# Forty-four tiny loads added to a decode kernel that streams its KV cache

## The chip, the cores and the metric

The kernel runs on one core of a Trainium2 chip. The metric is device time in microseconds (us); lower is better. The kernel before takes 1275.87 us (median of three runs, 1275.85 to 1275.99). Five engines run their own instruction streams: TensorE (PE in the profile, with PEld for its weight loads), VectorE (DVE), ScalarE (ACT), GpSimd (POOL) and SyncE (SP). Data moves between main memory and the on-chip SBUF through 16 DMA engines; a load is issued by an instruction on one of the five engines and announces its landing by raising a semaphore by 16.

## The reference, cut to what matters

One token of an attention block with a long cache and one token of a gated feed-forward block are computed from the same input and mixed by a gate:

```python
x = A_x                                                   # 1 x 1 x 448
g = sigmoid((x * gate_w).sum(-1, keepdims=True))
q = (x @ wq)                                              # 16 heads of 256
scores = einsum("bhqd,bhkd->bhqk", q, k) * 256 ** -0.5    # 65536 cached keys, 8 KV heads
a = (softmax(scores) @ v) @ wo                            # 16*256 -> 448
b = ((relu(x @ W_gate)) * (x @ W_up)) @ W_down
return g * a + (1 - g) * b
```

The K cache and the V cache are 8 heads x 65536 x 256 values in bfloat16 each, 268 MB each. Everything else together is some 12 MB. So nearly all that the kernel does is to read 537 MB once.

## The kernel before, in words

K and V are read in tiles of 128 partitions x 32768 values (64 KB in a partition, 8.4 MB in all). There are 32 K tiles and 32 V tiles, four of each for a KV head; K tile `n` belongs to head `n // 4`. Three SBUF buffers, `ring0` to `ring2`, hold them. K tiles go alternately to `ring1` and `ring2`, V tiles to `ring0`; the last V tiles also use `ring1` and `ring2`, and the very last one comes in three pieces (`vp`, line 776).

All of these loads, and those of the weights, are issued by SyncE, in one fixed order (the list `order`): K0, `wq`, K1, `W_down`, K2, the gate and up weights, K3, and then K4, V0, K5, V1 and so on in pairs. The V tile `n - 4` stands right behind the K tile `n`. At the end stand the last V tiles, the three pieces of V31, six loads of `wo` in falling size (line 785), and the store of the output (line 798).

What a tile goes through:

- A K tile lands; VectorE transposes it in place in four pieces (line 529); TensorE multiplies it with the query into a PSUM bank `ST` (line 540, in two halves, `qk[n, 0]` and `qk[n, 1]`); VectorE takes the maximum (line 703), ScalarE the exponential (line 705). When `qk[n, 1]` is done, the buffer is free, and SyncE may issue K tile `n + 2` into it (line 680).
- A V tile lands; ScalarE copies the probabilities that belong to it (`pcur`, line 591); TensorE multiplies (line 584, `pv[n]`) into the PSUM bank `O`. When `pv[n]` is done, SyncE may issue the next V tile into `ring0` (line 772).

The order of the work is written by hand. Each operation has an engine, a key (a planned time) and the operations on which it depends; each engine's program is its operations sorted by key (`_Plan.finish`), and a dependency becomes a wait on a semaphore in front of the instruction (`_Plan.emit`). An instruction that waits holds all that stand behind it on its engine. `l_["xm"]` is the spread-out query, an early operation on VectorE. `scr` is a scratch tile of 128 x 1024 values that is used in the first 50 us only. GpSimd builds constants in the first 7 us and then has nothing left to do.

Of the kernel before, what the change touches and what calls it, by code (L numbers as in the profile page):

```python
# [27 lines left out]
class _Plan:  # L28
# [8 lines left out]
    def op(self, eng, key, fn, deps=(), tag=None):  # L37
        eng, cls = {"pv": ("pe", "pv"), "dx": ("dv", "dx"), "ap": ("ac", "ap")}.get(eng, (eng, eng))
        o = _Op(eng, key, fn, deps, tag=tag, cls=cls)
        self.ops.append(o)  # L40
        return o

    def dma(self, eng, key, sem, fn, deps=()):
        if sem not in self.dsem:
            self.dsem[sem] = self.es.enter_context(self.nc.semaphore("d_" + sem))
        o = _Op(eng, key, fn, deps, dma=sem)
        self.ops.append(o)
        return o
# [212 lines left out]
def bass_gated_mix__gqa_block_cached__glu_gated_reglu__decode_kernel(  # L261
# [35 lines left out]
    with es:  # L297
# [7 lines left out]
        scr = sb("scr", [128, 1024], BF)  # L305
        xcur = sb("xcur", [128, 136], BF)
        xm = sb("xm", [128, H * 128 + 8], BF)
# [32 lines left out]
        fin_o = P_sb[0:1, 0:D]  # L340
# [30 lines left out]
        op, dma = pl.op, pl.dma  # L371
# [23 lines left out]
        t = 3.0  # L395
# [5 lines left out]
        T_END = t + 20.0  # L401
# [115 lines left out]
        def k_src(n):  # L517
            h, t_ = divmod(n, NTH)
            return A_k_cache[0, h, t_ * TK:(t_ + 1) * TK, :].rearrange("(p u) d -> p (u d)", u=U)

        def v_src(i):
            h, a = divmod(i, NTH)
            return A_v_cache[0, h, :, :].rearrange("(t g p u) d -> g p t (u d)", t=NTH, g=NTH, u=U)[a]
# [37 lines left out]
        l_, qk, smax, aexp, pv, pc, last, first = {}, {}, {}, {}, {}, {}, {}, {}  # L561
        pending = []

        def free(key):
            out_ = []
            for f in freed[key]:
                out_.append(l_[f] if isinstance(f, str) else qk[f[1], 1] if f[0] == "k" else pv[f[1]])
            return out_
# [55 lines left out]
        for kind, i, t in sorted(issue, key=lambda q: q[0] != "wq"):  # L624
# [51 lines left out]
            elif kind == "k":  # L676
                n = i
                h, t_ = divmod(n, NTH)
                sl = slot["k", n]
                kd = dma("sp", t, "r%d" % sl, lambda e, n=n, sl=sl: e.dma_start(ring[sl][:], k_src(n)), free(("k", n)))  # L680
                tk = max(tL["k", n], last.get("free", 0))
                tr = [op("dv", tk + 4.5 * w, f_trans(sl, w), [kd]) for w in range(4)]
# [25 lines left out]
                if t_ == NTH - 1:  # L708
# [18 lines left out]
                    for rd in range(2):  # L727
# [10 lines left out]
                        p = op("pe", tt + 0.5, f_ptr, [rsc, g_idb], tag=("ptr", rd))  # L738
# [29 lines left out]
            elif kind in ("v", "vp"):  # L768
                if kind == "v":
                    n, lo, hi = i, 0, U  # L770
                    sl = slot["v", n]
                    dep = dma("sp", t, "r%d" % sl, lambda e, sl=sl, n=n: e.dma_start(ring[sl][:], v_src(n)), free(("v", n)))
                else:
                    n, (lo, hi) = NT - 1, PIECES[i]
                    sl = slot["vp", 0]
                    dep = dma("sp", t, ("wq", "wqh", "wd")[i], lambda e, sl=sl, n=n, lo=lo, hi=hi: e.dma_start(  # L776
                        ring[sl][:, lo * 256:hi * 256], v_src(n)[:, :, lo * 256:hi * 256]), free(("vp", 0)))
                args = (n, lo, hi, sl, tL[kind, i], dep)
                if ("tev", n // NTH) in last:
                    make_pv(*args)  # L780
                else:
                    pending.append(args)
            elif kind == "wo":
                lo, hi = WO[i]
                l_["wo", i] = dma("sp", t, "wo%d" % i, lambda e, lo=lo, hi=hi: e.dma_start(  # L785
                    wo_sb[:, lo:hi, :], A_wo.rearrange("(p s) n -> p s n", s=32)[:, lo:hi, :]), free(("wo", 0)))

# [7 lines left out]
            fin = op("pv", max(LAST + 0.5 + i, tL["wo", i]), f_wo, [l_["wo", i], aA, l_["dn"]])  # L795
        f0 = op("dx", T_END, lambda e: e.tensor_copy(fin_o[:, 0:D2], A_ps[0:1, 0:D2]), [fin])
        f1 = op("ap", T_END, lambda e: e.copy(fin_o[:, D2:D], A_ps[32:33, 0:D2]), [fin])
        f2 = dma("sp", T_END + 1, "out", lambda e: e.dma_start(out[0, :, :], fin_o), [f0, f1])

        pl.serialize(touch_m)  # L800
        for o in touch_m:
# [74 lines left out]
```

## Time and profile before

| what | value |
|---|---|
| median of three runs | 1275.87 us (1275.85 to 1275.99) |
| span of the profiled execution, first to last instruction | 1274.3 us |
| what the device time has around that span | some 1.6 us |
| TensorE busy | 365.9 us (29%) |
| VectorE busy | 630.1 us (49%) |
| ScalarE busy | 78.0 us (6%) |
| GpSimd busy | 4.6 us |
| bytes read | 549.03 MB, 431 GB/s over the span |
| mean granted TensorE clock | 0.634 |

The profile's page gives busy times, a strip of the span in 40 slices, the DMA queues, the chain of work that ended last, and the costliest groups of instructions. `SPq` is the time in which SyncE issues a load: a row `SPq L772` tells of the instruction that starts a transfer, not of the transfer. `q1` is the queue of the loads that SyncE issues; its packets are single runs of data and the small writes that raise a semaphore. `DMA ring<-in_A_v_cache_dram` in the chain is time in which the next step waited for a V tile to land.

### The profile page before, as it was taken

The page shows a single profiled execution, that of the slowest core. Times are in us where ns is not written, and L with a number is a line of the kernel's source. Part 1 is how long each engine was busy: PE and PEld are TensorE (multiplying, and loading weights), DVE is VectorE, ACT ScalarE, POOL GpSimd, SP SyncE. Part 2 cuts the span into 40 slices and gives each one's busy share as a digit, 9 for nine tenths or more (in the row PEclk, how much of TensorE's full clock was granted, in tenths as well). Part 3 has the DMA queues.
Part 4 walks back from the last instruction along what each step waited for, and adds up shares of the span by engine and source line. Part 5 has one row for each costly group of instructions (what it writes and reads, how often), then busy time and mean ns, then how long its engine had stood idle before and what let it go on. Part 6 is the DMA issues. An engine that isn't in the chain of part 4 may idle for free.

```text
span 1274.3 us, 10240 instructions
## 1 busy us (share of the span) xinstructions
PE 365.9 (29%) x4497; PEld 151.4 (12%) x4505; DVE 630.1 (49%) x309; ACT 78.0 (6%) x163; POOL 4.6 (0%) x23
## 2 busy tenths in 40 slices
PE   0534321133320332312233222323302332112525
PEld 0101110011110111101111110111100111001201
DVE  4777655553455633557433565335654355553300
ACT  0001100010000100001000010000000010000100
POOL 1000000000000000000000000000000000000000
PEclk9766665666655666656666656666566666566667
DMA  9999999999999999999999999999999999999998
GB/s 411 430 436 432 426 430 434 432 443 432 430 432 432 434 442 430 430 434 430 438 438 430 430 434 430 440 438 428 430 434 430 444 434 428 430 436 430 442 421 369
DMA packets 11389, 549.13 MB, mean 431 GB/s; under 512 B 1267, under 2 KB 1654, under 8 KB 2294
## 3 DMA queue, kind: packets, MB, share of 16 engines
q1 hardware_dynamic: 11378, 549.03, 99.7%
q8 instruction: 4, 0.07, 0.0%
q14 instruction: 3, 0.02, 0.0%
q10 hardware_dynamic: 4, 0.00, 0.0%
HBM read 549.03 MB, written 0.00 MB: 431 GB/s over the span
## 4 chain that ended last, share of the span: by engine, by line
DMA 81%; PE 16%; DVE 2%; ACT 1%; issue 1%; SPq 0%; ACTq 0%
DMA ring<-in_A_v_cache_dram 74%; PE O L584 13%; DMA ring<-in_A_wo_dram 3%; DMA ring<-in_A_wq_dram 2%; DMA ring<-in_A_k_cache_dram 2%; DVE ring L529 1%; PE ST L540 1%; ACT pcur L591 1%; PE O L501 1%; PE A_ps L551 0%; SPq L785 0%; SPq L776 0%; PE O L653 0%; DVE ring L660 0%; PE A_ps L653 0%
## 5 line engine op out<-in xcount | busy, mean ns | idle before, releaser
L529 DVE STREAM_TRANSPOSE ring<-ring 128x4096 uint32<-128x4096 uint32 x128 | 557.6, 4413 | 196.9 <-DMA ring<-in_A_k_cache_dram 196.9
L584 PE MATMUL O<-ring,pcur 128*4 128x512 bf16 x2048 | 187.3, 545 | 790.4 <-ACT pcur L591 781.9
L703 DVE TENSOR_REDUCE nmb<-ST 128x1 f32<-128x512 f32 x32 | 22.1, 692 | 345.9 <-PE ST L540 345.9
L584 PEld LDWEIGHTS O<-ring,pcur 128*4 128x4 bf16 x2048 | 59.3, 111 | 914.8 <-ACT pcur L591 794.6
L540 PE MATMUL ST<-ring,xcur 128*16 128x512 bf16 x2048 | 136.7, 420 | 44.3 <-DVE ring L529 43.7
L540 PEld LDWEIGHTS ST<-ring,xcur 128*16 128x16 bf16 x2048 | 62.4, 92 | 112.1 <-DVE ring L529 48.6
L705 ACT ACTIVATE P_sb<-ST,nmb 128x512 bf16<-128x512 f32 x32 | 44.6, 1392 | 368.3 <-DVE nmb L703 368.3
L591 ACT COPY pcur<-ptp 128x256 bf16<-128x256 bf16 x32 | 13.2, 415 | 732.6 <-DMA ring<-in_A_v_cache_dram 732.6
L607 DVE TENSOR_SCALAR o_sb<-O,rcm 128x256 bf16<-128x256 f32 x8 | 3.8, 479 | 61.1 <-PE O L584 61.1
L730 DVE TENSOR_TENSOR P_sb<-P_sb,hs 128x1024 bf16<-128x1024 bf16 x16 | 18.9, 1222 | 8.1 <-ACT hs L724 8.1
L735 PE MATMUL PT<-identb,P_sb 128*128 128x128 bf16 x128 | 14.5, 282 | 17.6 <-DVE P_sb L730 17.3
L501 PE MATMUL O<-ring,P_sb 128*128 128x512 bf16 x28 | 8.5, 477 | 17.3 <-DMA ring<-in_A_wq_dram 17.3
L735 PEld LDWEIGHTS PT<-identb,P_sb 128*128 128x128 bf16 x128 | 10.7, 127 | 19.9 <-DVE P_sb L730 19.9
L744 ACT COPY ptp<-PT 128x256 bf16<-128x256 bf16 x32 | 10.3, 375 | 23.0 <-PE PT L735 23.0
L705 ACT ACTIVATION_READ_ACCUMULATOR P_sb<-ST,nmb 128x1 f32 x32 | 8.3, 258 | 0.0
L501 PEld LDWEIGHTS O<-ring,P_sb 128*128 128x128 bf16 x28 | 3.2, 117 | 22.2 <-issue 20.5
L551 PE MATMUL A_ps<-ring,attnA 128*1 128x224 bf16 x64 | 5.3, 322 | 1.1 <-DMA ring<-in_A_wo_dram 1.0
L719 PE MATMUL M_ps<-identf,hs 128*2 128x128 f32 x8 | 2.3, 283 | 10.0 <-DVE hs L717 10.0
L756 DVE RECIPROCAL rc<-M_ps 128x2 f32<-128x2 f32 x8 | 1.4, 171 | 7.5 <-PE M_ps L755 7.5
L755 PE MATMUL M_ps<-hs,ones_f 128*128 128x2 f32 x16 | 4.5, 352 | 0.0
L722 PE MATMUL M_ps<-mx,nselT 2*128 2x1 f32 x16 | 3.2, 268 | 3.0 <-DVE mx L721 3.0
L755 PEld LDWEIGHTS M_ps<-hs,ones_f 128*128 128x128 f32 x16 | 4.0, 311 | 0.0
(93 smaller groups left out, 68.6 us busy)
## 6 DMA issues: line engine op xcount, KB each, us to landing
ring<-in_A_v_cache_dram SPq DMA_DIRECT2D x1, 4096.0 KB, 22.1
ring<-in_A_wq_dram SPq DMA_DIRECT2D x1, 3072.0 KB, 28.9
ring<-in_A_v_cache_dram SPq DMA_DIRECT2D x1, 3072.0 KB, 28.8
ring<-in_B_W_down_dram SPq DMA_DIRECT2D x1, 1568.0 KB, 53.0
ring<-in_B_W_gate_dram SPq DMA_DIRECT2D x1, 1344.0 KB, 26.3
ring<-in_B_W_up_dram SPq DMA_DIRECT2D x1, 1344.0 KB, 29.2
ring<-in_A_wo_dram SPq DMA_DIRECT2D x1, 1232.0 KB, 33.0
ring<-in_A_v_cache_dram SPq DMA_DIRECT2D x1, 1024.0 KB, 30.7
```

The lines of the kernel that those rows point to most:

```text
L501: ins = e.matmul(QN_ps, xw3[:, kt, 31 - m:159 - m], rhs, start=(kt == 0 and m == 0), stop=(kt == R3 and m == J // 4 - 1))
L529: return lambda e: e.transpose(v, v)
L540: ins = e.matmul(bank[32 * w:32 * w + 16, :], xcur[:, x0:x0 + 16], ktv[sl][:, u0:u0 + 16, c, :, r_], start=(b == 0 and c == 0 and r_ == 0) ...
L551: ins = e.matmul(A_ps[32 * g:32 * g + 1, 0:D2], lhsT, rhs[:, g * D2:(g + 1) * D2], start=start, stop=stop, skip_group_check=True, tile_pos ...
L584: ins = e.matmul(OP[32 * g:32 * g + 4, :], pcur[a % 2][:, 4 * k:4 * k + 4], ring[sl][:, k * 512:(k + 1) * 512], start=False, stop=False, s ...
L591: pc[n] = op("ap", max(tp - 5, last["tev", h] - 0.5), lambda e: e.copy(pcur[a % 2][:].rearrange("p (k i) -> p k i", i=4), ptp[:].rearrange ...
L703: smax[n] = op("dv", sx, lambda e, n=n, t_=t_: e.tensor_reduce(NM[:, t_:t_ + 1], ST[n % 2][:], AX.X, ALU.max, negate=True), [qk[n, 1], las ...
L705: aexp[n] = op("ac", sx + 1, lambda e, n=n, t_=t_: e.activation(P_sb[:, t_:2048:4], ST[n % 2][:], ACTF.Exp, bias=NM[:, t_:t_ + 1], scale=1 ...
L730: rsc = op("dv", tt, lambda e, pb=pb: e.tensor_tensor(pb, pb, X[:, 12:16].unsqueeze(1).to_broadcast([128, 256, 4]), ALU.mult), [h7, aexp[n]])
L735: ins = e.transpose(PT[rd][:, s * 128:(s + 1) * 128], P_sb[:, (rd * 8 + s) * 128:(rd * 8 + s + 1) * 128], identb[:, :])
L744: ins = e.copy(dst, src)
L755: l3 = mop("pe", T + 19, lambda e: e.matmul(LS_ps, ones_f[:, :], X[:, 6:8], start=True, stop=True), [l2, c_one], tag="l3")
```

## The change

Forty-four small loads are added, all from `B_W_gate` into `scr`, which nothing reads any more by then.

- Fifteen by SyncE just ahead of K8, the ninth K tile. Load `j` (1 to 15) takes `j` partitions of `32 + 2j` values: 68 to 124 bytes in a partition. They wait for `xm`.
- Fourteen by GpSimd, behind its last constant. They wait for `qk[9, 1]` and `xm`. Each takes 2 partitions (three of them 3, 5 and 8), two separate runs of 200 to 252 bytes in each.
- Fifteen more by SyncE, like the first, between the last piece of V31 and the first load of `wo`. The first of them waits until the earlier fifteen have landed.
- The store of the output gets two more waits, for the second fifteen and for GpSimd's fourteen.

SyncE's program around K8, before (the names are buffers and inputs; `[waits ...]` names the semaphores waited for, `s_pe` and `s_pv` those of TensorE):

```order
L680 DMA ring2<-in_A_k_cache_dram 128x32768 [waits s_pe]
L772 DMA ring0<-in_A_v_cache_dram 128x1x32768 [waits s_pv]
L680 DMA ring1<-in_A_k_cache_dram 128x32768 [waits s_pe]
L772 DMA ring0<-in_A_v_cache_dram 128x1x32768 [waits s_pv]
L680 DMA ring2<-in_A_k_cache_dram 128x32768 [waits s_pe]
```

The first two rows are K7 and V3, the third is K8. The same place now, where line 689 is the new one, 691 the K loads and 783 the V loads:

```order
L691 DMA ring2<-in_A_k_cache_dram 128x32768 [waits s_pe]
L783 DMA ring0<-in_A_v_cache_dram 128x1x32768 [waits s_pv]
L689 DMA scr<-in_B_W_gate_dram 1x34 [waits s_dx]
L689 DMA scr<-in_B_W_gate_dram 2x36
L689 DMA scr<-in_B_W_gate_dram 3x38
...
L689 DMA scr<-in_B_W_gate_dram 14x60
L689 DMA scr<-in_B_W_gate_dram 15x62
L691 DMA ring1<-in_A_k_cache_dram 128x32768 [waits s_pe]
L783 DMA ring0<-in_A_v_cache_dram 128x1x32768 [waits s_pv]
```

So K8 is issued behind fifteen more instructions, and the small loads stand in SyncE's queue between the data of V3 and that of K8.

The end of SyncE's program before, from the last piece of V31 on:

```order
L776 DMA ring2<-in_A_v_cache_dram 128x1x4096
L785 DMA ring0<-in_A_wo_dram 128x4928
L785 DMA ring0<-in_A_wo_dram 128x3136
L785 DMA ring0<-in_A_wo_dram 128x2240
L785 DMA ring0<-in_A_wo_dram 128x1792
L785 DMA ring0<-in_A_wo_dram 128x1344
L785 DMA ring0<-in_A_wo_dram 128x896
L798 DMA out_0_dram<-P_sb 1x448 [waits s_ap,s_dx]
```

The same place now:

```order
L787 DMA ring2<-in_A_v_cache_dram 128x1x4096
L799 DMA scr<-in_B_W_gate_dram 1x34 [waits d_probe]
L799 DMA scr<-in_B_W_gate_dram 2x36
...
L799 DMA scr<-in_B_W_gate_dram 15x62
L801 DMA ring0<-in_A_wo_dram 128x4928
L801 DMA ring0<-in_A_wo_dram 128x3136
L801 DMA ring0<-in_A_wo_dram 128x2240
L801 DMA ring0<-in_A_wo_dram 128x1792
L801 DMA ring0<-in_A_wo_dram 128x1344
L801 DMA ring0<-in_A_wo_dram 128x896
L814 DMA out_0_dram<-P_sb 1x448 [waits d_probe,d_probe1,s_ap,s_dx]
```

All six `wo` loads stand behind fifteen more instructions, and the store has two more waits. On TensorE, VectorE and ScalarE no instruction moves; on GpSimd the fourteen loads stand behind all that it had.

```diff
                 sl = slot["k", n]
+                if n == 11:
+                    for j, k_ in enumerate((2, 2, 2, 2, 2, 2, 2, 2, 3, 5, 2, 8, 2, 2)):
+                        w_ = 100 + 2 * j
+                        l_["probe2"] = dma("gp", t + 0.001 * j, "probe1", lambda e, j=j, w_=w_, k_=k_: e.dma_start(
+                            scr[32 + 8 * (j % 12):32 + 8 * (j % 12) + k_, 320 * (j // 12):320 * (j // 12) + 320].rearrange("p (s w) -> p s w", s=2)[:, :, 0:w_],
+                            B_W_gate[0:k_, 0:320].rearrange("p (s w) -> p s w", s=2)[:, :, 0:w_]), [qk[9, 1], l_["xm"]])
+                if n == 8:
+                    for j in range(1, 16):
+                        w_, o_ = 32 + 2 * j, 31 * j + j * j - 32
+                        l_["probe"] = dma("sp", t - 0.1 + 0.001 * j, "probe", lambda e, j=j, w_=w_, o_=o_: e.dma_start(
+                            scr[0:j, o_:o_ + w_], B_W_gate[0:j, 0:w_]), [l_["xm"]])
                 kd = dma("sp", t, "r%d" % sl, lambda e, n=n, sl=sl: e.dma_start(ring[sl][:], k_src(n)), free(("k", n)))
...
                 lo, hi = WO[i]
+                if i == 0:
+                    for j in range(1, 16):
+                        w_, o_ = 32 + 2 * j, 31 * j + j * j - 32
+                        l_["probe3"] = dma("sp", t - 0.1 + 0.001 * j, "probe", lambda e, j=j, w_=w_, o_=o_: e.dma_start(
+                            scr[0:j, o_:o_ + w_], B_W_gate[0:j, 0:w_]), [l_["probe"]])
                 l_["wo", i] = dma("sp", t, "wo%d" % i, lambda e, lo=lo, hi=hi: e.dma_start(
...
-        f2 = dma("sp", T_END + 1, "out", lambda e: e.dma_start(out[0, :, :], fin_o), [f0, f1])
+        f2 = dma("sp", T_END + 1, "out", lambda e: e.dma_start(out[0, :, :], fin_o), [f0, f1, l_["probe3"], l_["probe2"]])
```

## The prediction

> **What bounds the kernel now.** I read the page's busy times and strip first, then the chain, then the stages by windows, then SyncE's issues around the two places of the change. The page:
>
> ```profile
> PE 365.9 (29%) x4497; PEld 151.4 (12%) x4505; DVE 630.1 (49%) x309; ACT 78.0 (6%) x163; POOL 4.6 (0%) x23
> DMA  9999999999999999999999999999999999999998
> DMA packets 11389, 549.13 MB, mean 431 GB/s; under 512 B 1267, under 2 KB 1654, under 8 KB 2294
> q1 hardware_dynamic: 11378, 549.03, 99.7%
> DMA 81%; PE 16%; DVE 2%; ACT 1%; issue 1%; SPq 0%; ACTq 0%
> ```
>
> No engine is busy for more than half of the span, while the sixteen DMA engines are full in every slice and SyncE's queue fills 99.7% of their time. The 16% of PE in the chain are only the links between one V load and the next issue. The stages (columns: time, then busy time of each engine, granted clock, DMA share, GB/s):
>
> ```profile
> core 0: us, PE busy (x) PEld busy (x) DVE busy (x) ACT busy (x) POOL busy (x), PEclk, DMA share, GB/s
> 104.00:225.00 121.00, 34.74 (x419) 13.90 (x422) 74.13 (x30) 7.59 (x17) 0.00 (x0) 0.62 1.00 433
> 225.00:263.24 38.24, 9.24 (x136) 3.78 (x128) 18.12 (x5) 1.81 (x3) 0.00 (x0) 0.64 1.01 437
> 1195.00:1231.68 36.68, 15.84 (x169) 6.21 (x160) 5.52 (x14) 3.97 (x10) 0.00 (x0) 0.63 1.01 435
> ```
>
> At both places of the change the DMA share is 1.00 or more. So two things alone can cost time: work added to the DMA engine that finishes last, and a pause in which the queue runs dry. Whatever is late on SyncE or GpSimd costs nothing as long as the queue holds data.
>
> **Fifteen loads ahead of K8: the issues.** SyncE around K8, the chain over the same time, and VectorE's first work on K8:
>
> ```profile
> 225.11 0.55 SPq L772 DMA_DIRECT2D ring<-in_A_v_cache_dram  x1
> 228.79 0.33 SPq L680 DMA_DIRECT2D ring<-in_A_k_cache_dram  x1
> 263.24 0.55 SPq L772 DMA_DIRECT2D ring<-in_A_v_cache_dram  x1
> ```
>
> ```profile
> 225.11 32.08 DMA ring<-in_A_v_cache_dram
> ```
>
> ```profile
> 276.56 17.42 DVE L529 STREAM_TRANSPOSE ring<-ring 128x4096 uint32<-128x4096 uint32 x4 [1.48 <-DMA ring<-in_A_k_cache_dram]
> ```
>
> V3 is issued at 225.11 and lands at 257.19; K8 is issued at 228.79 and lands at about 276.6. K8's data begin to flow when V3's end, at about 257, so its issue has 257.2 - 229.1 = 28 us in hand. The small loads do not wait: `xm` was ready before the first scores. Their price on SyncE is bounded by single issues at the end of the program:
>
> ```profile
> 1231.68 1.83 SPq L776 DMA_DIRECT2D ring<-in_A_v_cache_dram  x3
> 1233.55 8.72 SPq L785 DMA_DIRECT2D ring<-in_A_wo_dram  x6
> 1273.11 0.32 SPq L798 DMA_DIRECT2D out_dram<-P_sb  x1
> ```
>
> The store of one row took 0.32 us, a 128-row load 1.83 / 3 = 0.61 us. Fifteen cost 4.8 to 9.2 us; I take 0.4 each, 6 us, nearer to the one-row issue. SyncE then reaches K8 at 225.66 + 6 = 231.7 instead of 228.79: 3 us late, of 28 in hand. V4, next in line, is not issued before 263.24 in any case. If the cover of 28 us were gone, the 3 us would show whole. Cost: 0.
>
> **The same fifteen: the DMA engines.** The two packets of the one-row store, data of 896 bytes and its completion write, in a window of 0.4 us:
>
> ```profile
> DMA packets 2, 0.00 MB, mean 2 GB/s; under 512 B 1, under 2 KB 2, under 8 KB 2
> q1 hardware_dynamic: 2, 0.00, 0.8%
> ```
>
> 0.8% of 16 engines x 0.4 us is 0.05 us for the pair. The added runs are 68 to 124 bytes, so 0.05 us is an upper price for one run with its completion. No view shows how a small load is shared out, so I bound it: the worst is an engine that takes part in all fifteen, 15 x 0.05 = 0.77 us; the best is that the engine concerned has time to spare. That it may, the completions of one V tile show (windows 390.2 to 390.9 and 391.3 to 392.3; the strip has 40 slices of each window):
>
> ```profile
> DMA  0009900090009090000900009000000900009000
> DMA packets 22, 0.72 MB, mean 1030 GB/s; under 512 B 11, under 2 KB 11, under 8 KB 11
> ```
>
> ```profile
> DMA  0009000000000000000000090900900000900000
> DMA packets 10, 0.33 MB, mean 328 GB/s; under 512 B 5, under 2 KB 5, under 8 KB 5
> ```
>
> Packets under 512 bytes are the completions here. Eleven engines are through a tile by 390.83 (slice 36 of the first strip), the last of the other five at 392.15 (slice 34 of the second). Eleven of sixteen are thus 1.3 us or more ahead of the engine that ends last, and all work at the same pace, as the queue is never empty. On one of the eleven, 0.77 us vanishes; on the last it counts whole. I take 0 (eleven in sixteen) and keep 0.77.
>
> The Trainium skill has a rule for this place. DMA: Bandwidth & Descriptors, section "Why a DMA increments its semaphore by 16 and not by 1", says that a load uses the largest number of engines up to 16 that divides its outer dimension, and on this path the lowest-numbered ones. By it the first engine takes a share of all fifteen loads, 0.77 us, where an even spread of the 120 runs would make 120 / 16 x 0.05 = 0.4 us. No run here shows yet which engine that is.
>
> **Fifteen loads ahead of wo.** The same two prices. SyncE would begin the `wo` loads at 1233.55 + 6 = 1239.6. When their data are first wanted shows in the last piece of V31:
>
> ```profile
> 1263.61 0.18 PEld L584 LDWEIGHTS O<-ring,pcur 128*4 128x4 bf16 x8 [0.68 <-DMA ring<-in_A_v_cache_dram]
> ```
>
> It landed at 1263.6, so the issue has 24 us in hand: cost 0. The wait of the first of them on the earlier fifteen is long over. On the DMA engines again 0 to 0.77 us; together with the first set 1.5 us at most, and of that all but some 0.2 us hides on an engine that leads by 1.3.
>
> **Fourteen loads by GpSimd.** They use another queue and are off every chain: GpSimd is idle (0.00 in the windows above), and the one waiter is the store at the end, 900 us later. They bring 38 partitions x 2 runs x 226 bytes, 17 KB, which at 433 GB/s is 0.04 us, and completions. Bounds per engine: 0, and 14 x 0.05 = 0.7 us if one engine has a part in every load. I take 0.2.
>
> **The two added waits of the store.** Both are long satisfied. The steps between instructions in the chain there are 0.04 us:
>
> ```profile
> 1272.24 0.04 issue
> ```
>
> 2 x 0.04 = 0.08 us, on the path that ends the kernel. Bounds 0 and 0.2.
>
> **Sum.** 0 + 0 + 0.2 + 0.1 = 0.3 us on a span of 1274.3, so 1274.6; what lies around the span (1275.87 - 1274.3 = 1.6) stays. Forecast 1276.2 against the median of 1275.87. With every upper bound: 1.5 + 0.7 + 0.2 = 2.4 us, 1278.3. Both are within 0.2% (2.55 us), which is about what a measurement of this kernel can tell from no change.
>
> **Rival 1, slower: SyncE's queue takes only so many loads.** One issue in the trace did wait without a semaphore. In the chain:
>
> ```profile
> 1236.01 0.33 SPq L785
> 1236.35 0.05 issue
> 1236.40 35.84 DMA ring<-in_A_wo_dram
> ```
>
> Five `wo` loads were issued by 1236.35, and the group of six above ends at 1233.55 + 8.72 = 1242.27: the sixth took 5.9 us. The next V tile landed two us later:
>
> ```profile
> 1244.15 0.74 ACT L591 COPY pcur<-ptp 128x256 bf16<-128x256 bf16 x2 [18.94 <-DMA ring<-in_A_v_cache_dram]
> ```
>
> So at 1236.4 nine loads were pending (V30, three pieces, five of `wo`), and the tenth came in about when V30 ended on most engines. That is either a limit on packets or one on loads. If on packets: each of those loads has 8 runs and a completion on an engine, so 9 x 9 = 81 were pending when the tenth had come in without V30. At K8 the fullest engine would hold K7, V3, the small loads and K8, 9 + 9 + 30 + 9 = 57: no wait. Ahead of `wo` it would hold 27 + 30 + 54 = 111; SyncE is held, but each `wo` load comes in as the pieces drain, with the earlier ones already queued. Cost 0. The skill's page Perfetto Trace Analysis, section on the HWDGE DMA instruction, speaks of a descriptor buffer that fills while the issuing instruction lasts; by that it is packets.
>
> If it is loads, with nine pending: at K8, K7 and V3 and seven small ones fill it; the eighth enters as K7 ends and the ninth as V3 ends; then the engines are dry while six small loads (6 x 0.32), K8's issue (0.33) and the start of its data (at most 0.8, from the store's issue end at 1273.43 to the end of the span) go by: 3.1 us. Ahead of `wo`, in the same way behind the last piece: 6 x 0.32 + 0.59 + 0.8 = 3.3 us. Sum 6.4, time 1282.3. It decides from a limit under some seventeen loads on. For it: the 5.9 us. Against it: eighty packets explain them as well.
>
> **Rival 2, slower: small loads are served one after another.** If each held its engine until it had landed, a load would cost up to that same 0.8 us. Thirty make 24 us, less the lead of 1.3: time 1298. Against it the six `wo` loads (window 1263.6 to 1272.3):
>
> ```profile
> DMA  9998999999989999898999999999986543232000
> DMA packets 787, 2.91 MB, mean 335 GB/s; under 512 B 96, under 2 KB 224, under 8 KB 736
> ```
>
> 96 completions, six on each engine, pass with no gap until the engines run out of work. But there a completion stands behind several KB, here behind 68 bytes; that keeps the rival alive. The skill (DMA: Bandwidth & Descriptors, "Anatomy of one DMA") puts a fixed 2.0 us on a load, most of it the wait for the write's receipt; thirty of those in a row would be an estimated 60 us.
>
> **Rival 3, faster: the last engine's lag changes.** The five late engines lost their 1.3 us or more to something outside the loads; a longer program on two engines may move that. It gives at most the lag, 1.3 to 1.9 us: time 1274, still within 0.2%.
>
> **How the numbers follow.** Forecast with its bounds, rival 3 included: 0.77 (of that 0.04 below 1275.4). Rival 1: 0.14. Rival 2, or a part of it: 0.06. A gain over 0.2% has no mechanism in the rows; 0.03 for what I do not see. So same 0.77, slower 0.20, faster 0.03. The range must hold 8 in 10: from 1275.4, below which only a shift of the lag leads, to 1280.0, which takes in all upper bounds and part of rival 1 and 2 (a lower limit of either cost).
>
> **What would show it.** Right: the issue of K8 moves to about 232 while its data still land near 276.6; DMA share 1.00 in the stretch 225 to 300; the `wo` loads still end 8.6 us after V31's last piece; the chain still runs through V tiles. Wrong: a stretch of low DMA share at about 257 or 1263 of 3 us each with SyncE's issues behind it (rival 1), or K8 landing some 10 us late on one engine with the others ahead (rival 2).

## The result and the profile after

The changed kernel takes 1278.93 us (median of 8 runs, 1278.62 to 1279.78) against 1275.93 us (8 runs, 1275.81 to 1276.00): 3.0 us more. The ratio is 1.0024 with a 95% interval of 1.0013 to 1.0035, so it is slower, clear of the noise. By the median it is just beyond the 0.2% that the prediction drew as its line; the interval reaches to both sides of that line. The time lies in the predicted range; the forecast of no change, 1276.2, misses it by 2.7 us.

The page of the changed kernel, its DMA rows and its chain:

```profile
DMA packets 12317, 549.17 MB, mean 430 GB/s; under 512 B 2195, under 2 KB 2582, under 8 KB 3222
q1 hardware_dynamic: 11858, 549.06, 99.6%
q0 software_dynamic: 448, 0.02, 0.0%
DMA 79%; PE 15%; SPq 2%; DVE 2%; ACT 1%; issue 1%; ACTq 0%
```

SyncE's queue has 480 packets more (11858 - 11378): two sets of 120 runs and 120 completions. GpSimd's queue `q0` has 448, which is 14 x 32: just what two packets of each load on each of the sixteen engines make. The queue is still 99.6% full. Where did 3 us go? First, SyncE around K8 and at the end:

```profile
225.23 0.54 SPq L783 DMA_DIRECT2D ring<-in_A_v_cache_dram  x1
225.81 5.43 SPq L689 DMA_DIRECT2D scr<-in_B_W_gate_dram  x15
231.28 0.39 SPq L691 DMA_DIRECT2D ring<-in_A_k_cache_dram  x1
...
1234.42 5.40 SPq L799 DMA_DIRECT2D scr<-in_B_W_gate_dram  x15
1239.86 21.66 SPq L801 DMA_DIRECT2D ring<-in_A_wo_dram  x6
1276.04 0.27 SPq L814 DMA_DIRECT2D out_dram<-P_sb  x1
```

Fifteen small loads are issued in 5.4 us, without a stop. K8 is issued 2.5 us later than before and still 25 us before V3 has landed. So the issues cost nothing at K8. The chain over the V tiles ahead of and behind K8, after:

```profile
225.23 31.79 DMA ring<-in_A_v_cache_dram
...
263.37 33.41 DMA ring<-in_A_v_cache_dram
```

and the second of them before:

```profile
263.24 32.65 DMA ring<-in_A_v_cache_dram
```

V3 lands at 257.02 (257.19 before), V4 at 296.78 (295.89 before). From 0.17 us early to 0.89 us late: 1.06 us are lost between them. Bytes that the DMA engines began in the window 254 to 260, before and then after:

```profile
DMA packets 61, 2.95 MB, mean 492 GB/s; under 512 B 16, under 2 KB 16, under 8 KB 16
```

```profile
DMA packets 294, 2.50 MB, mean 417 GB/s; under 512 B 256, under 2 KB 256, under 8 KB 256
```

Behind V3 the engines begin fewer bytes although nothing is missing in the queue. At the end, TensorE's start on V31's last piece and the chain behind it:

```profile
1264.92 0.18 PEld L584 LDWEIGHTS O<-ring,pcur 128*4 128x4 bf16 x8 [0.67 <-DMA ring<-in_A_v_cache_dram]
```

```profile
1260.84 14.35 DMA ring<-in_A_wo_dram
1275.19 0.04 issue
```

The last piece lands 1.31 us later than before (1264.92 against 1263.61). From there to the landing of the last `wo` load it is 10.27 us; before, it was 1272.24 - 1263.61 = 8.63. So 1.3 us are lost by then, and 1.64 us more behind the second set: 2.95, the whole difference.

### The profile page after: what moved, and what is told of

Same layout as the page of the kernel before. It is cut to its first block, busy times and chain, and to the rows that moved or that the text cites. A ratio compares the mean times of both kernels' runs of the same rounds, so it can differ in the third digit from the quotient of the medians.

```text
span 1277.2 us, 10286 instructions
## 1 busy us (share of the span) xinstructions
PE 360.4 (28%) x4497; PEld 149.0 (12%) x4505; DVE 630.1 (49%) x309; ACT 77.9 (6%) x163; POOL 12.6 (1%) x37
## 3 DMA queue, kind: packets, MB, share of 16 engines
q1 hardware_dynamic: 11858, 549.06, 99.6%
## 4 chain that ended last, share of the span: by engine, by line
DMA 79%; PE 15%; SPq 2%; DVE 2%; ACT 1%; issue 1%; ACTq 0%
DMA ring<-in_A_v_cache_dram 74%; PE O L584 13%; DMA ring<-in_A_wq_dram 2%; DMA ring<-in_A_k_cache_dram 2%; SPq L801 2%; DVE ring L529 1%; DMA ring<-in_A_wo_dram 1%; PE ST L540 1%; ACT pcur L591 1%; PE O L501 1%; SPq L799 0%; PE A_ps L551 0%; SPq L787 0%; PE O L653 0%; PE A_ps L653 0%
## 5 line engine op out<-in xcount | busy, mean ns | idle before, releaser
L584 PE MATMUL O<-ring,pcur 128*4 128x512 bf16 x2048 | 183.2, 535 | 795.6 <-ACT pcur L591 789.1
L683 POOL DMA_DIRECT2D scr<-in_B_W_gate_dram x14 | 8.0, 577 | 339.1 <-PE ST L540 339.1
```

The source lines that it names most:

```text
L584: ins = e.matmul(OP[32 * g:32 * g + 4, :], pcur[a % 2][:, 4 * k:4 * k + 4], ring[sl][:, k * 512:(k + 1) * 512], start=False, stop=False, s ...
L683: l_["probe2"] = dma("gp", t + 0.001 * j, "probe1", lambda e, j=j, w_=w_, k_=k_: e.dma_start(scr[32 + 8 * (j % 12):32 + 8 * (j % 12) + k_, ...
```

## The experiments

All keep the kernel before and change only the added loads, for which the store at the end waits. Times are medians of 11 runs (one has 5), beside 27 to 33 runs of the kernel before on the same chip, which give 1275.93 to 1275.96. The interval of a ratio is some 0.0009 to each side (1.1 us), wider than most steps between the experiments; the runs of one experiment lie within 0.8 us, so I read steps of half a microsecond from medians whose runs do not overlap, and say where they do. By the interval alone five kernels are clear of no change: both sets together, fifteen and thirty loads on 16 partitions, the 1 KB rows and the semaphores of their own. Each set alone just touches it (1.0000 to 1.0018), and the other five include it.

| kernel | median, us | runs, us | over before |
|---|---|---|---|
| first set alone | 1277.04 | 1276.87 to 1277.25 | 1.08 |
| second set alone | 1277.10 | 1276.87 to 1277.31 | 1.14 |
| GpSimd's loads alone | 1276.27 | 1276.21 to 1276.43 | 0.31 |
| both sets, no GpSimd | 1278.66 | 1278.36 to 1279.10 | 2.73 |
| 15 loads on two partitions | 1276.78 | 1276.60 to 1277.03 | 0.82 |
| 15 loads on 16 partitions | 1278.19 | 1278.04 to 1278.61 | 2.24 |
| 1 load of 16 x 15 runs | 1276.19 | 1276.03 to 1276.83 | 0.24 |
| 15 loads, one ahead of each K tile | 1276.43 | 1276.24 to 1276.58 | 0.48 |
| 30 loads on 16 partitions | 1281.74 | 1281.36 to 1281.88 | 5.79 |
| 5 loads on 16 partitions | 1276.12 | 1275.84 to 1276.32 | 0.19 |
| 15 loads of 1 KB rows | 1278.70 | 1278.49 to 1279.01 | 2.77 |
| 15 loads, a semaphore each | 1278.12 | 1277.86 to 1278.47 | 2.19 |

**One part alone.** The first set, the second set, GpSimd's loads; what is kept of the diff:

```diff
+                if n == 8:
+                    for j in range(1, 16): ...            # first kernel: SyncE ahead of K8
...
+                if i == 0:
+                    for j in range(1, 16): ...            # second kernel: SyncE ahead of wo
...
+                if n == 11:
+                    for j, k_ in enumerate((2, 2, ...)): ...   # third kernel: GpSimd
```

> Only the fifteen loads ahead of K8 are left of the change. Theory A (each engine pays some 0.13 us for each small load in a row beyond the first three or so, and the engine that is last after that sets the end; in the changed kernel V tiles land 1.07 us later from here on): 1275.93 + 0.9 to 1.3, so 1276.8 to 1277.2. Theory B (small loads cost only the time of their packets, at most 0.05 us each, and the 3 us came from the loads ahead of wo or from a longer program): within 0.3 of 1275.93.

> Only the fifteen loads ahead of wo are left of the change. Theory A: 1275.93 + 0.9 to 1.7, so 1276.8 to 1277.6, the span's last stretch behind V31's last piece longer by as much. Theory B, with the pause in SyncE's issues: more, 2 to 3 us.

> Only GpSimd's fourteen loads are left of the change. In the changed kernel V tiles land 0.4 us later behind them than ahead of them. Theory A, and theory B too: 1275.93 + 0.2 to 0.5. If a program on GpSimd that issues loads costs something outside the stream (start or end), over 0.5.

All three as theory A had it: 1.08, 1.14 and 0.31 us. GpSimd's runs overlap with those of before (up to 1276.49), so 0.3 us is about as much as can be told from nothing. Theory B's 0.3 for the first set is out, and so are its 2 to 3 us for the second. V31's last piece in the kernel with the first set and in the one with the second:

```profile
1264.54 0.18 PEld L584 LDWEIGHTS O<-ring,pcur 128*4 128x4 bf16 x8 [0.67 <-DMA ring<-in_A_v_cache_dram]
```

```profile
1263.26 0.18 PEld L584 LDWEIGHTS O<-ring,pcur 128*4 128x4 bf16 x8 [0.67 <-DMA ring<-in_A_v_cache_dram]
```

Before, it was at 1263.61. The first set has delayed it by 0.9 us, the second (which stands behind it) has not.

The three sum to 2.53, the change costs 3.0. So one more run left out GpSimd's loads alone:

> Both sets of fifteen by SyncE, without GpSimd's loads. If the sets simply add up: 1275.95 + 1.08 + 1.14 = 1278.17. If the second set costs more once the first has used up the lead of the engines that carry most loads: 1278.4 to 1278.8, and GpSimd's fourteen are then worth the 0.3 us that they cost alone.

1278.66: 2.73, not 2.22. The second set costs more when the first has gone ahead. In the profiles, from V31's last piece to VectorE's last copy it takes 1273.40 - 1263.26 = 10.14 us with the second set alone and 10.55 with both, against 9.07 before:

```profile
1272.68 0.38 DVE P_sb L796
```

```profile
1273.40 0.38 DVE P_sb L801
```

```profile
1264.53 0.18 PEld L584 LDWEIGHTS O<-ring,pcur 128*4 128x4 bf16 x8 [0.67 <-DMA ring<-in_A_v_cache_dram]
```

```profile
1275.08 0.38 DVE P_sb L806
```

(The first row is of the kernel before, the second of the second set alone, the others of both.) That is what one expects if the same engines carry most of both sets and the first set uses up their lead.

**Which engines carry the loads.**

```diff
-                            scr[0:j, o_:o_ + w_], B_W_gate[0:j, 0:w_]), [l_["xm"]])
+                            scr[0:2, o_:o_ + w_], B_W_gate[0:2, 0:w_]), [l_["xm"]])
```

> In place of all added loads, fifteen ahead of K8 that all take two partitions. If a load of j partitions keeps to the same j engines, two engines carry all fifteen. Theory A with the lead of the early engines: those two lose some 1.9 us and lead by up to 1.9, so 1275.93 + 0 to 0.4. If the loads went round the engines, or if the time is lost on all engines together (issue, queue), as much as with the fifteen ahead of K8 of one to fifteen partitions, 0.9 to 1.3.

```diff
+                            scr[0:16, o_:o_ + w_], B_W_gate[0:16, 0:w_]), [l_["xm"]])
```

> In place of all added loads, fifteen ahead of K8 of sixteen partitions each, so that every engine may have one run of each. Theory A: all engines lose some 1.9 us, the last one too: 1277.5 to 1278.1. Theory B (packet times): 0.2 to 0.8 us, 1276.1 to 1276.7.

On sixteen partitions 2.24 us: 1278.19, just above the range that I expected. On two partitions 0.82: a miss for the 0 to 0.4 that I expected. The median lies below the 0.9 to 1.3 of the rival, but the runs overlap with those of the first set (1276.87 and up), so the time alone does not rule it out. The profile does. The kernel with two partitions, window 253.9 to 256.9, in which K8's data begin behind the row:

```profile
DMA packets 94, 1.18 MB, mean 394 GB/s; under 512 B 76, under 2 KB 76, under 8 KB 76
q1 hardware_dynamic: 94, 1.18, 100.2%
```

Sixteen of the 76 small packets are the completions of V3. The other 60 are four for each of the fifteen loads: two runs and two completions. So a load of two partitions has a part on two engines only. The last column is the time that the packets begun in the window took, as a share of sixteen engines. A narrow window in the same profile, 255.005 to 255.060:

```profile
DMA packets 8, 0.13 MB, mean 2388 GB/s; under 512 B 6, under 2 KB 6, under 8 KB 6
q1 hardware_dynamic: 8, 0.13, 977.6%
```

Two 64 KB packets begin in it, 0.055 us apart at most and thus on two engines. They take 977.6% of 16 x 0.055 us, 8.6 us: 4.3 us each. For the sixteen other 64 KB packets of the longer window 2.4 us each are left (100.2% of 48 us is 48.1, less 8.6 and some 0.8 for the small ones). So two engines lost 1.9 us in the packet behind the row, and the other fourteen nothing. With the row's own packets, 15 x 0.02 us (the price is read off below), these two lost some 2.2 us, of which the kernel was spared 1.4: about the lead of 1.3 us or more that the prediction read from the completions of a V tile. So the loads do stay on the same few engines, as the Trainium skill says (DMA: Bandwidth & Descriptors, "Why a DMA increments its semaphore by 16 and not by 1"); the runs agree with that rule, but no view here names an engine.

**What of a small load costs.**

```diff
+                if n == 8:
+                    l_["probe"] = dma("sp", t - 0.1, "probe", lambda e: e.dma_start(
+                        scr[0:16, 0:960].rearrange("p (s w) -> p s w", s=15)[:, :, 0:48],
+                        B_W_gate[0:16, 0:960].rearrange("p (s w) -> p s w", s=15)[:, :, 0:48]), [l_["xm"]])
```

> One load ahead of K8 of sixteen partitions with fifteen runs of 96 bytes in each: as many runs on an engine as with fifteen loads of sixteen partitions, but one completion instead of fifteen. If the runs of data are what costs: as those fifteen, 1277.5 to 1278.1. If runs and completions count alike: half of it, about 1276.9. If the completions cost: 1275.9 to 1276.1.

0.24 us (1276.19, just above the 1276.1 expected), a tenth of what the same number of runs costs in fifteen loads; the times overlap with those of before. Runs of data are nearly free. What costs is the number of loads in a row, each with a completion of its own. In the window 253.9 to 256.9, fifteen loads of sixteen partitions and then the single load:

```profile
DMA packets 515, 1.27 MB, mean 423 GB/s; under 512 B 496, under 2 KB 496, under 8 KB 496
q1 hardware_dynamic: 515, 1.27, 172.5%
```

```profile
DMA packets 290, 1.20 MB, mean 401 GB/s; under 512 B 272, under 2 KB 272, under 8 KB 272
q1 hardware_dynamic: 290, 1.20, 101.9%
```

By the last column, 172.5% of 48 us is 82.8, against 48.9. Of the 33.9 us between them one more 64 KB packet is 2.4. For the 224 more small packets even half of the 0.05 us pair would be 5.6. At least 26 us are left, 1.6 us for each engine. They must lie in K8's first packets, which had begun behind the small ones and took longer, as on the two engines above.

```diff
+                if 8 <= n < 23:
+                    j = n - 7
+                    ...                                    # one load of 16 partitions
```

> The fifteen loads of sixteen partitions, but one ahead of each of the K tiles 8 to 22 instead of all ahead of K8. Theory A (only what stands in a row beyond the first three or so costs): 1276.0 to 1276.4. If each load costs its 0.13 us wherever it stands: 1277.5 to 1278.1.

The same fifteen loads one at a time cost 0.48 us (the runs overlap with those of before, up to 1276.41), 0.03 each, close to what their packets take. It is just above the 1276.4 expected. Only a row of them costs. How the row's length counts:

```diff
-                    for j in range(1, 16):
+                    for j in range(1, 31):                 # and in another kernel range(1, 6)
...                                                         # loads 16 to 30 go to partitions 32 to 47
```

> Thirty loads of sixteen partitions ahead of K8. Theory A, in a straight line: 0.13 us for each of 27, so 3.5 us, 1279.4. If the price has a ceiling (a gap that is paid once, as when an engine has to begin again): as with fifteen, 1277.5 to 1278.1.

> Five loads of sixteen partitions ahead of K8. With the knee (0.19 us for each load beyond four, and the packets' own 0.02 each): 1275.95 + 0.2 = 1276.1 to 1276.3. In proportion to fifteen (2.24 / 3): 1276.7.

Five cost 0.19 us, fifteen 2.24, thirty 5.79. Five are hardly to be told from none; from five to fifteen it is 0.21 us a load, from fifteen to thirty 0.24. There is no ceiling; thirty came out 2.3 us above the straight line that I had drawn with 0.13. It is not SyncE that is late with thirty:

```profile
225.56 14.01 SPq L684 DMA_DIRECT2D scr<-in_B_W_gate_dram  x30
239.61 0.42 SPq L686 DMA_DIRECT2D ring<-in_A_k_cache_dram  x1
```

K8 is issued at 239.6, 17 us before V3's end at 257. Where the time goes instead, two windows of the same profile show, 254.85 to 255.09 and 255.09 to 255.46:

```profile
DMA packets 298, 0.01 MB, mean 62 GB/s; under 512 B 298, under 2 KB 298, under 8 KB 298
q1 hardware_dynamic: 298, 0.01, 84.4%
```

```profile
DMA packets 168, 0.66 MB, mean 1794 GB/s; under 512 B 158, under 2 KB 158, under 8 KB 158
q1 hardware_dynamic: 168, 0.66, 1249.9%
```

The first holds small packets alone: 84.4% of 16 x 0.24 us is 3.24 us for 298 of them, 0.011 us each, so some 0.02 us for a run with its completion, in the middle of a row. In the second, ten 64 KB packets of K8 begin. They take 74.0 us (1249.9% of 16 x 0.37) less 1.7 for the small ones: 7.2 us each instead of 2.4. So the small loads themselves pass quickly, and the price of the row is paid in the packet behind it: 4.8 us more behind thirty loads, 1.9 behind fifteen.

```diff
+                    for j in range(15):
+                        p_, o_ = 16 * (j // 2), 512 * (j % 2)
+                        ...   scr[p_:p_ + 16, o_:o_ + 512], B_W_gate[p_:p_ + 16, o_:o_ + 512]
```

> Fifteen loads ahead of K8 of sixteen partitions with 1024 bytes in each, ten times the bytes of the fifteen that made 1278.19. Their data alone are 15 x 16 KB, 0.57 us at 433 GB/s. If a completion holds its engine until its data are confirmed, and the next data flow meanwhile: as with the small ones, 1278.0 to 1278.4. If data and holding add up: 1278.6 to 1278.9.

Ten times the bytes: 0.53 us more, 2.77 against 2.24. The bytes alone are 0.57 us. So by the medians data and holding add up, though the two kernels' runs overlap a little (1278.49 and up here, up to 1278.61 there).

```diff
-                        l_["probe"] = dma("sp", t - 0.1 + 0.001 * j, "probe", ...
+                        l_["probe%d" % j] = dma("sp", t - 0.1 + 0.001 * j, "probe%d" % j, ...
```

> The fifteen loads of sixteen partitions ahead of K8 with a semaphore of their own each, instead of one for all. If the completions of one semaphore hinder one another: 1276.4 or less. If each engine waits for its own write before the completion may go out, whatever the semaphore: 1278.0 to 1278.5, with up to 0.6 us more for the fourteen additional waits ahead of the store.

2.19 us: the shared semaphore is not the cause, and fourteen more waits ahead of the store show no cost.

## Why the prediction was right or wrong

**What bounds the kernel: right.** The queue stayed full, and the time was lost on the DMA engines alone. But a full queue is no proof that data flow: a packet that takes 4.3 us instead of 2.4 counts as busy for all of them, and the share of the changed kernel stayed at 99.6%.

**The issues ahead of K8 and of wo, cost 0: right.** 6 us were predicted for fifteen, 5.4 came; the time in hand covered them. K8's issue moved to 231.28, as forecast; the `wo` loads ended 10.27 us behind V31's last piece and not 8.6, which was the sign that the DMA term was wrong.

**The small loads on the DMA engines: wrong, and this is the step that failed.** "0.05 us is an upper price for one run with its completion" was taken from one pair of packets that stood alone, and for the pair's own time it holds: 0.02 us in the middle of a row. But the sum took that to be the whole price and had no term for the packet behind the row. That packet took 1.9 us longer behind fifteen loads on its engine, 4.8 behind thirty; beyond about the fifth load in a row each cost its engine some 0.2 us. So the bound "15 x 0.05 = 0.77 us" of the worst engine was in truth 2.2 us, three times as much. The second half of the step failed with it: "I take 0 (eleven in sixteen)" set the whole set on one engine with a lead. The loads of one to fifteen partitions reach many engines, and a lead of 1.3 us cannot hide what the later ones lose. The lead itself was real: with the loads on two engines, 1.4 of some 2.2 us vanished. In the sum, 0 for the first set measured 1.08 us, and 0 for the second 1.14 alone and some 1.6 behind the first.

**The range held by its margin, and not by the sum.** With every upper bound the sum came to 1278.3, below all eight runs of the changed kernel (1278.62 and up). The range reached on to 1280.0 only to take in a part of rivals 1 and 2. That the time lies in it is luck, as far as the sum goes.

**GpSimd's fourteen, 0.2 us: about right, as far as it can be told** (0.31 alone, 0.27 as the step from 1278.66 to 1278.93; in both the runs overlap). Their packets go through a queue of their own and are spread over some 60 us of the stream, which would explain why they do not act as a row (the changed kernel, windows 349 to 380 and 380 to 411):

```profile
q0 software_dynamic: 227, 0.01, 0.5%
```

```profile
q0 software_dynamic: 221, 0.01, 0.5%
```

**The two waits ahead of the store, 0.1 us: not to be seen.** From the end of VectorE's last copy to the store it was 0.05 us (1273.06 to 1273.11) and is 0.03 (1276.01 to 1276.04).

**Rival 1, a limit on loads in SyncE's queue: out.** Fifteen small loads behind K7 and V3, and in an experiment thirty, were issued without a stop, so nine pending loads are no limit. K7 had landed by 237.74, when VectorE began on it, and the last of the thirty was issued at 239.57, so V3 and thirty loads were pending. At the end SyncE was held, as the reading by packets said. The chain names three of its issues:

```profile
1240.76 7.36 SPq L801
1248.17 7.25 SPq L801
1255.46 5.34 SPq L801
```

But the last of the six was in at 1239.86 + 21.66 = 1261.5, before V31's last piece had landed. The page of the Trainium skill that speaks of a filling buffer (Perfetto Trace Analysis, "DMA Instruction — HWDGE (DVE, Sync)") fits a hold by packets. That this hold cost nothing is argued: the second set alone costs 1.14 us with it, the first alone 1.08 without a hold at K8.

**Rival 2, small loads served one after another: the nearest to what happened, at a quarter of its price.** It had up to 0.8 us for each load and no free ones; the runs have about 0.2 us behind the first four or five. That each load holds its engine until it has landed is not shown: the packets of a row pass at some 0.02 us a load, and the time is lost in the packet behind them. (Its own sum, 1275.87 + 24 - 1.3, is 1298.6 and not 1298.) It had 0.06 of the chances. The evidence that I set against it, 96 completions of `wo` without a gap, came from loads with half a microsecond and more of data on each engine between two completions, and the prediction said that this kept it alive; it should have been priced between the ends, not put aside. The Trainium skill's page DMA: Bandwidth & Descriptors ("Anatomy of one DMA") says two things that the runs take apart: that the write of the semaphore is itself nearly free, which holds for one completion behind fifteen runs (0.24 us in all), and that it waits for the data before it, which is what a row of loads would pay each time. That section is written for loads that GpSimd issues, and no run here shows such a wait by itself.

**What stays open.** Why the packet behind the row is held, no run tells. "The completions wait for their own data, and what is behind waits for them" is a reading that fits one cheap load of fifteen runs, the added 0.5 us of larger rows and the semaphores of their own; a fixed cost of each load that the engine pays behind the row would fit them too. Why the first four or five are free was not tried either; that an engine still has data in hand then is only argued.

## What to carry to other kernels

A stream that keeps the DMA engines full has little slack for a row of tiny loads: price them by the number of loads in a row that an engine takes part in (here some 0.2 us for each beyond the first five), not by bytes or packets. Put them one at a time between large loads, or merge them into one load with many runs, and they cost little (here 0.48 and 0.24 us for fifteen). When an isolated event gives a price, check the price of a row of them before it is multiplied.

## What the hardware showed that was not expected

- A 64 KB packet that takes 2.4 us in the stream took 4.3 us behind fifteen tiny loads on its engine and 7.2 behind thirty, while the tiny packets themselves took 0.011 us each.
- Fifteen loads of 16 short rows in a row cost 2.24 us of stream and thirty 5.79; the same runs as one load cost 0.24, and one load ahead of each of fifteen K tiles 0.48.
- SyncE issued thirty loads in 14 us, and K8 behind them, without being held: with V3 up to 9 + 60 packets on an engine, 78 with K8. Ahead of `wo`, with more pending, the third to fifth of the six took 7.36, 7.25 and 5.34 us to issue. The hold does not go by loads; by packets it would lie at around eighty on an engine, an estimate from these counts and the 81 of the prediction.
- Each of GpSimd's loads, of two partitions mostly, made 32 packets (448 for 14), which fits a part for all sixteen engines; a load by SyncE of two partitions made four (60 for 15).
